# Eight heads per tile: sliding-window K and V loaded in 64 KB rows, each tile in two 64-partition transfers

## The chip, the cores and the metric

The kernel runs on one core of one Trainium2 chip; the chip's other cores are not used. The metric is the device time of the program in microseconds. The kernel is written in Bass with a recording layer of its own: every operation is recorded with what it reads and writes, semaphores are worked out from that, and then each engine's list is emitted in the recorded order. Five engines take part: TensorE (PE, with its weight loads as PEld), VectorE (DVE), ScalarE (ACT), GpSimd (POOL) and SyncE (SP). SP does nothing but issue the large loads, in program order, each behind its waits.

## The reference

Two independent attention layers, A and B, decode one token, and their outputs are concatenated. Both have 32 heads of width 128, a model width of 512, and caches of 16,384 positions in bfloat16. A attends to all positions, B only to the last 4,096.

```python
def _B_ref(x, k_cache, v_cache, wq, wo):           # A: the same with W = Sk
    W = min(4096, max(256, Sk // 4))
    q = (x @ wq) ... [heads, 1, 128]
    k, v = k_cache[:, :, Sk - W:, :], v_cache[:, :, Sk - W:, :]
    scores = einsum("bhqd,bhkd->bhqk", q, k) * (Dh ** -0.5)
    o = einsum("bhqk,bhkd->bhqd", softmax(scores), v)
    return o.reshape(B, Sq, Hq * Dh) @ wo

return concatenate([A(...), B(...)], axis=-1)
```

K and V are read once: A has 2 x 134.2 MB, B 2 x 33.6 MB in its window (67.1 MB in all), and the four weight matrices 4.2 MB each.

## The kernel before

**Units and tiles.** The work is cut into 20 units, each with a K tile and a V tile of 8 MB: 128 partitions, 256 positions (`2 * CH`) of 128 values per partition. A unit of A holds two heads: 64 partitions each, and a partition holds 256 consecutive positions of one head, a 64 KB row of the cache. A has 16 units. A unit of B holds eight heads as two parts of four: part `u` is positions `u * CH` to `(u + 1) * CH` of the tile's free dimension, and within it partition `4 * i + h` holds 128 positions of head `h`, a 32 KB row. B has 4 units. The order of units is B0, then A0 to A15, then B1 to B3.

**Buffers.** Two K buffers (`KS`) in turn, and one V buffer (`VS`). An 8 MB tile of A is one DMA transfer; a tile of B is two of 4 MB, one for each part (`b_window`, `load_k_half`, `load_k`, `load_v`). The first unit's two K parts are loaded around A's `wq`, the last unit's V parts go one into the free K buffer (`VL0`, behind A's `wo`) and one into `VS` (`VL1`), and B's `wo` follows in five pieces of 16, 8, 4, 3 and 1 rows (`wo_pieces`, line 765).

**What a unit does.** DVE multiplies K by the head's q in two products (`scores_prod`, line 437, one for each half of the free dimension), adds up along the 128 values in a tree of four additions (line 449) and a reduction (line 456), and takes the maximum per partition (line 465). PE turns the maxima into a row, DVE takes the maximum per head and spreads it (`max_all`, lines 488 and 489), PE turns it back. ACT makes the exponentials with their sums (line 516) and writes them into `pm` once for each head of the tile, masked so that a head keeps only its own partitions (`spread_p`, line 502). PE multiplies `pm` by V (`pv`, line 564), ACT scales and evicts (line 576), PE picks the heads' columns (`columns`, line 586), ACT stores them (line 595). The softmax and PV of a unit are recorded between the two products and the tree of the next unit.

**What a load waits for.** K of unit T + 1 waits until DVE has finished the tree of unit T - 1 (`free_k`, line 461). V of unit T - 1 is issued after the column store of unit T - 2 (line 595), so that VS is free. SP's order is V of T - 1, K of T + 1, V of T, and so on. In a unit of B, the first product waits for the first K transfer alone, the second product for the second; PV waits for both V transfers.

**The end.** The last unit's V is multiplied the other way round, into columns (`pv_columns`, line 604), part 0 from the K buffer into `oc_t`, part 1 from `VS` into `OC2`, each normalised by DVE (line 611). Then the heads' outputs are permuted (`permute_o`), multiplied by `wo` piece by piece (line 656), summed (line 665), turned (line 669) and stored.

Of the kernel before, what the change touches and what calls it, by code (L numbers as in the profile page):

```python
# [12 lines left out]
P = 128  # L13
# [18 lines left out]
class _Stream:  # L32
# [13 lines left out]
    def __init__(self, tc):  # L46
        self.tc, self.nc = tc, tc.nc
        nc = tc.nc
        self.eng = {"PE": nc.tensor, "DVE": nc.vector, "ACT": nc.scalar, "SP": nc.sync, "POOL": nc.gpsimd}
        self.ops = {e: [] for e in self.eng}  # L50
        self.known = {e: {} for e in self.eng}
        self.writer, self.readers = {}, {}
        self.sems, self.tokens, self.counts, self.taken = {}, {}, {}, set()
        self.loop = {}

    def sem(self, name):
# [16 lines left out]
    def op(self, eng, emit, r=(), w=(), dma=None, tok=None, takes=()):  # L73
        assert all(k in self.writer or "." in k for k in r), r
        known = self.known[eng]
# [152 lines left out]
def kernel(  # L228
# [21 lines left out]
    inv = 1.0 / math.sqrt(DH)  # L250
    assert SkA == P // 2 * 2 * CH and WB == P // 4 * CH

# [15 lines left out]
    ident = sb("ident", [P, P], BF16)  # L268
    one_f = sb("one_f", [1, 1], F32)
    one_b = sb("one_b", [1, 1], BF16)  # L270
    ones_col = sb("ones_col", [P, 1], F32)
    pick = sb("pick", [HQ, P + 4], BF16)
    sc = sb("sc", [P, 2 * CH], F32)
    m_t = sb("m", [P, 2], F32)
    M_t = sb("M", [1, 8], F32)
    Mr = sb("Mr", [1, 2 * P], F32)
    bias = sb("bias", [P, 2], F32)
    p_t = sb("p", [P, 2 * CH], BF16)
    cs = sb("cs", [P, 2], F32)
    csm = sb("csm", [P, 8], F32)  # L280
    pm_t = sb("pm", [P, 2 * CH * 4], BF16)
    r_t = sb("r", [P, 8], F32)
# [7 lines left out]
    A, B = _Side(), _Side()  # L290
    for s, n, x, wq, wo, nh in ((A, "A", A_x, A_wq, A_wo, 2), (B, "B", B_x, B_wq, B_wo, 4)):
        s.n, s.x, s.wq, s.wo, s.nh, s.parts = n, x, wq, wo, nh, nh // 2
        s.xT = sb(f"xT{n}", [P, KC], BF16)
        s.q = sb(f"q{n}", [P, HQ // nh, DH], BF16)
        s.O = sb(f"O{n}", [P, HQ], BF16)
        s.Op = sb(f"Op{n}", [P, HQ], BF16)
        s.mask = sb(f"mask{n}", [P, nh], F32)
        s.groups = 4 // s.parts
        s.rows = sb(f"rows{n}", [P, 8 * s.groups // nh, nh, 4], F32)
        s.sel = sb(f"sel{n}", [P, s.parts, nh * 4], F32)  # L300
        s.o = pst(f"o{n}")
# [6 lines left out]
    def by_head(s, ap):  # L308
        if s is A:
            return ap.rearrange("p (h i) -> p h i", h=s.nh)  # L310
        return ap.rearrange("p (i h) -> p h i", h=s.nh)

    def b_window(cache, g):
        return cache[0, 4 * g : 4 * g + 4, SkB - WB : SkB, :].rearrange("h (i l) d -> i h (l d)", l=CH)

# [18 lines left out]
    def load(dst, src, w, dma, tok=None):  # L334
        st.op("SP", lambda: L.dma_start(out=dst, in_=src), w=w, dma=dma, tok=tok)  # L335

    def load_k_half(un, u):
        load(flat(un.K[:, u * CH : (u + 1) * CH, :]), b_window(B_k_cache, 2 * un.g + u),
             [f"k{un.k}{u}"], f"K{un.k}{u}")

    def load_k(un):
        if un.s is A:
            load(flat(un.K[:, :, :]), a_pair(A_k_cache, un.g), [f"k{un.k}0", f"k{un.k}1"], f"K{un.k}0")
# [24 lines left out]
    def make_masks(s):  # L368
        n = s.n
        st.op("DVE", lambda: V.tensor_reduce(out=s.mask[:, :], in_=by_head(s, identf[:, :]), axis=AX.X, op=ALU.add),  # L370
              r=["identf"], w=["mask" + n])
# [11 lines left out]
    def spread_x(s, area, key):  # L383
# [16 lines left out]
        for j in range(s.nh):  # L400
            dst = s.xb[:, j, :, :]
            if s is A:
                dst = dst.rearrange("p c (h i) -> p c h i", h=s.nh)[:, :, j, :]
            else:
                dst = dst.rearrange("p c (i h) -> p c i h", h=s.nh)[:, :, :, j]
            st.op("DVE", lambda dst=dst: V.tensor_copy(dst, s.xT[:, :].unsqueeze(2).broadcast_to([P, KC, P // s.nh])),
                  r=["xT" + s.n, key], w=[f"{key}.{j}"])
# [20 lines left out]
    def scores_prod(un, u):  # L428
        s = un.s
        k = un.K[:, u * CH : (u + 1) * CH, :]  # L430
        j = un.g if s is A else 2 * un.g + u
# [44 lines left out]
    def max_all(un):  # L476
        s, n = un.s, un.s.parts
        w = n * s.nh
        if s is A:
            rows, wide = by_head(s, sm[0:1, 0:P]), by_head(s, Mr[:, 0:P])  # L480
            Mv = M_t[:, 0:w]
            spread = Mv.unsqueeze(2).broadcast_to([1, s.nh, P // s.nh])
        else:
            rows = sm[0:1, 0 : n * P].rearrange("p (v i h) -> p v h i", v=n, h=s.nh)
            wide = Mr[:, 0 : n * P].rearrange("p (v i h) -> p v h i", v=n, h=s.nh)
            Mv = M_t[:, 0:w].rearrange("p (v h) -> p v h", v=n)
            spread = Mv.unsqueeze(3).broadcast_to([1, n, s.nh, P // s.nh])
        st.op("DVE", lambda it=None: V.tensor_reduce(out=Mv, in_=rows, axis=AX.X, op=ALU.max), r=["sm_r"], w=["M"], takes=["smr"])  # L488
        st.op("DVE", lambda it=None: V.tensor_copy(wide, spread), r=["M"], w=["Mr"], tok="Mr")

        def turn():
            for v in range(n):
                i = T_.matmul(  # L493
                    sm[:, 256 + v : 257 + v], lhsT=Mr[:, v * P : (v + 1) * P], rhs=one_f[:, :],
                    start=True, stop=True,
                )
            return i

        st.op("PE", turn, r=["Mr", "one_f"], w=["sm_c"], takes=["Mr"], tok="smc")

# [55 lines left out]
    def pv(un):  # L556
# [14 lines left out]

        st.op("PE", mms, r=["v0", "v1"] + [f"pm0.{j}" for j in range(4)], w=["o" + s.n], takes=["V0"] if s is A else ["V0", "V1"], tok="pv")

# [24 lines left out]

    def pv_columns(un, v, V_t, vk, ps, pk, pmk, takes):
        s = un.s  # L600

        def mms():
            for l in range(un.n):
                x = T_.matmul(
                    ps[:, 0 : s.nh], lhsT=V_t[:, l, :], rhs=un.pm[:, (v * un.n + l) // 4, :, l % 4],
                    start=(l == 0), stop=(l == un.n - 1),
                )
            return x

        st.op("PE", mms, r=[vk] + [f"{pmk}.{j}" for j in range(4)], w=[pk], takes=takes)  # L610
        st.op("DVE", lambda: V.tensor_tensor(
            out=s.O[:, un.col(v) : un.col(v) + s.nh], in0=ps[:, 0 : s.nh],
            in1=r_t[:, v * s.nh : (v + 1) * s.nh], op=ALU.mult,
        ), r=[pk, "r"], w=[f"O{s.n}.{un.col(v)}"])

# [61 lines left out]

    x0 = 4 * KC * P
    x_pieces = ((0, D // 4), (D // 4, D // 2), (D // 2, D))
# [14 lines left out]
    ), r=["identf0"], w=["identf"])  # L694
    for t, key, val in ((one_f, "one_f", 1.0), (one_b, "one_b", 1.0), (ones_col, "ones_col", 1.0),
                        (A.o, "oA", 0.0), (B.o, "oB", 0.0)):
# [12 lines left out]
    st.op("SP", lambda: L.dma_start(out=flat(KS[1][:, :, :]), in_=a_pair(A_k_cache, 0)),  # L709
          w=["k10", "k11", *(f"x{n}.{a}" for n in "AB" for a, _ in x_pieces)] + [f"k10.{j}" for j in range(4)], dma="K10")  # L710

    parts = []
    for T, un in enumerate(units):
# [5 lines left out]
        if un.last:  # L719
# [55 lines left out]
    recip(un)  # L775
    pv_columns(un, 0, W[:, CH : 2 * CH, :], wk + "1", oc_t, "oc", "pm0", ["pm"])
# [38 lines left out]
```

## Time and profile before

The median of three runs is 824.38 us (824.25 to 824.51). The profiled execution took 824.25 us; its span, from the first to the last instruction, is 822.5 us.

| | |
|---|---|
| span of the profiled execution | 822.5 us |
| DVE busy | 750.4 us (91%) |
| PE busy | 197.9 us (24%), weight loads 99.0 us (12%) |
| ACT busy | 60.0 us (7%) |
| read from HBM | 352.32 MB |
| DVE products, lines 437 | 40 of 8.68 us |
| DVE trees, line 449 | 84 operations, 333.3 us |

How to read it: the page's second part cuts the span into 40 equal slices, and each digit is a busy share in tenths; its DMA row is the mean busy share of sixteen DMA engines, and the GB/s row what they moved. The list of DMA issues names tile and tensor, how many such transfers there were, their size, and the median time from issue to landing, which includes what stood ahead in the queue. In the chain that ended last, each step is followed back to what released it. The trace also keeps the packets of the DMA queues and the marks with which a transfer's sixteen shares report their completion. Timeline rows give start, duration, engine, line and operation.

### The profile page before, as it was taken

The numbers are of one execution on the slowest core, as the hardware profiler recorded it, in microseconds if no ns is written. First come the engines' busy times: TensorE is split into PE (matmuls) and PEld (weight loads), VectorE is DVE, ScalarE is ACT, GpSimd is POOL, SyncE is SP. The second block draws the span as 40 slices with busy tenths as digits, with TensorE's granted clock in tenths as the row PEclk, the third lists the DMA queues.
The fourth block names the chain that finished last, engine by engine and source line by source line (L and its number), as shares of the span: only waits on it lengthen the run. The fifth ranks groups of instructions, "written<-read, shape, count | busy, mean of one in ns | idle before, by whom it ended". The sixth has DMA issues, their size and how long they took to land. (4 is left out here: it accounts for less than half of the span.)

```text
span 822.5 us, 5105 instructions
## 1 busy us (share of the span) xinstructions
PE 197.9 (24%) x1985; PEld 99.0 (12%) x1985; DVE 750.4 (91%) x258; ACT 60.0 (7%) x168; POOL 0.7 (0%) x6
## 2 busy tenths in 40 slices
PE   3401212203030303030303212030303030303176
PEld 1100101101010101010101101010101010101035
DVE  2999899999999999999999999999999999999960
ACT  0101000001010100000000001010100000010111
POOL 0000000000000000000000000000000000000000
PEclk9765656565565655565655565555656555655575
DMA  9999999999999999999999999999999999999997
GB/s 383 433 433 433 457 412 450 418 447 421 444 424 441 427 437 430 437 430 437 430 437 430 437 430 437 430 437 430 437 430 437 430 422 445 422 433 431 432 432 298
DMA packets 8094, 352.44 MB, mean 429 GB/s; under 512 B 915, under 2 KB 1046, under 8 KB 1302
## 3 DMA queue, kind: packets, MB, share of 16 engines
q1 hardware_dynamic: 8072, 352.33, 99.2%
q8 instruction: 6, 0.10, 0.0%
q14 instruction: 2, 0.02, 0.0%
q10 hardware_dynamic: 14, 0.00, 0.0%
HBM read 352.32 MB, written 0.00 MB: 428 GB/s over the span
## 5 line engine op out<-in xcount | busy, mean ns | idle before, releaser
L449 DVE TENSOR_TENSOR k<-k 128x16384 bf16<-128x16384 bf16 (+3 forms) x84 | 333.3, 3968 | 2.2
L437 DVE TENSOR_TENSOR k<-k,qA 128x16384 bf16<-128x16384 bf16 x32 | 277.8, 8682 | 21.2 <-DVEq L122 21.1
L564 PE MATMUL oA<-v,pm 128*8 128x512 bf16 x1024 | 89.4, 525 | 111.0 <-PEq L122 111.0
L437 DVE TENSOR_TENSOR k<-k,qB 128x16384 bf16<-128x16384 bf16 x8 | 69.4, 8679 | 1.0 <-DVEq L122 1.0
L471 PE MATMUL sm<-identf,m 128*1 128x128 f32 x24 | 8.1, 369 | 207.8 <-PEq L122 207.8
L493 PE MATMUL sm<-one_f,Mr 1*128 1x1 f32 x48 | 12.4, 335 | 188.8 <-PEq L122 188.8
L564 PEld LDWEIGHTS oA<-v,pm 128*8 128x8 bf16 x1024 | 30.1, 110 | 163.7 <-issue 155.3
L456 DVE TENSOR_REDUCE sc<-k 128x256 f32<-128x2048 bf16 (+1 forms) x21 | 45.9, 2185 | 0.7
L493 PEld LDWEIGHTS sm<-one_f,Mr 1*128 1x128 f32 x48 | 11.2, 300 | 195.1 <-issue 195.1
L512 ACT ACTIVATE bias<-sm 128x1 f32<-128x1 f32 (+1 forms) x20 | 3.4, 171 | 412.0 <-ACTq L122 412.0
L471 PEld LDWEIGHTS sm<-identf,m 128*1 128x1 f32 x24 | 1.7, 80 | 209.7 <-issue 209.7
L576 ACT ACTIVATE osb<-oA,r 128x512 f32<-128x512 f32 x16 | 11.0, 687 | 214.1 <-ACTq L122 214.1
L564 PE MATMUL oB<-v,pm 128*16 128x512 bf16 x192 | 17.6, 546 | 23.1 <-PEq L122 23.1
L586 PE MATMUL oc<-selA,osb 128*128 128x2 f32 x128 | 16.4, 250 | 15.6 <-PEq L122 15.6
L586 PEld LDWEIGHTS oc<-selA,osb 128*128 128x128 f32 x128 | 15.5, 191 | 23.2 <-issue 23.2
L544 PE MATMUL sm<-cs,rowsA 128*128 128x1 f32 x32 | 8.9, 348 | 32.3 <-PEq L122 32.3
L502 ACT ACTIVATE pm<-p,maskA 128x256 bf16<-128x256 bf16 x32 | 14.5, 500 | 0.5
L544 PEld LDWEIGHTS sm<-cs,rowsA 128*128 128x128 f32 x32 | 8.0, 311 | 33.2 <-issue 33.2
L419 PE MATMUL tp<-v,osb 128*128 128x512 bf16 x32 | 9.1, 454 | 10.6 <-DMA v<-in_A_wq_dram 10.6
L516 ACT ACTIVATE p<-sc,bias 128x256 bf16<-128x256 f32 (+1 forms) x24 | 11.3, 470 | 0.6
L488 DVE TENSOR_REDUCE M<-sm 1x2 f32<-1x128 f32 (+1 forms) x20 | 6.0, 298 | 5.8 <-DVEq L122 5.8
L465 DVE TENSOR_REDUCE m<-sc 128x1 f32<-128x256 f32 (+1 forms) x20 | 8.4, 420 | 2.8
(73 smaller groups left out, 108.0 us busy)
## 6 DMA issues: line engine op xcount, KB each, us to landing
k<-in_B_k_cache_dram SPq DMA_DIRECT2D x8, 4096.0 KB, 35.9
v<-in_B_v_cache_dram SPq DMA_DIRECT2D x7, 4096.0 KB, 29.3
v<-in_B_wq_dram SPq DMA_DIRECT2D x1, 4096.0 KB, 12.2
v<-in_A_wq_dram SPq DMA_DIRECT2D x1, 4096.0 KB, 30.5
k<-in_A_wo_dram SPq DMA_DIRECT2D x1, 4096.0 KB, 33.5
k<-in_B_v_cache_dram SPq DMA_DIRECT2D x1, 4096.0 KB, 42.9
v<-in_B_wo_dram SPq DMA_DIRECT2D x1, 2048.0 KB, 25.1
v<-in_B_wo_dram SPq DMA_DIRECT2D x1, 1024.0 KB, 27.0
```

The costliest lines, as they stand in the source:

```text
L419: x = T_.matmul(out_ap, lhsT=s.xb[:, j, c, :], rhs=wq[:, c, j, g : g + 4, :], start=(k == 0), stop=(k == n - 1),)
L437: return V.tensor_tensor(out=k, in0=k, in1=s.q[:, bass.ds(i, 1), :].broadcast_to([P, CH, DH]), op=ALU.mult)
L449: st.op("DVE", lambda it=None, w=w: V.tensor_tensor(out=k[:, :, 0:w], in0=k[:, :, 0:w], in1=k[:, :, w : 2 * w], op=ALU.add), r=keys, w=keys)
L456: st.op("DVE", lambda it=None: V.tensor_reduce(out=sc[:, l0:l1], in_=un.K[:, l0:l1, 0:8], axis=AX.X, op=ALU.add), r=[f"k{un.k}{u}" for u i ...
L471: i = T_.transpose(sm[0:1, v * P : (v + 1) * P], m_t[:, v : v + 1], identf[:, :])
L493: i = T_.matmul(sm[:, 256 + v : 257 + v], lhsT=Mr[:, v * P : (v + 1) * P], rhs=one_f[:, :], start=True, stop=True,)
L502: return S.activation(out=out, in_=in_, func=ACT.Copy, scale=mask)
L516: st.op("ACT", lambda it=None, v=v: S.activation(out=p_t[:, v * n : (v + 1) * n], in_=sc[:, v * n : (v + 1) * n], func=ACT.Exp, scale=inv, ...
L544: i = T_.matmul(sm[v * w : (v + 1) * w, 264:265], lhsT=s.rows[:, :, :, :].rearrange("p r a b -> p (r a b)"), rhs=cs[:, v : v + 1], start=T ...
L564: x = T_.matmul(s.o[r0 : r0 + un.rows, :], lhsT=un.pm[:, l, :, :].rearrange("p a b -> p (a b)"), rhs=VS[:, 4 * l : 4 * l + 4, :], start=(i ...
L576: st.op("ACT", lambda it=None: S.activation(out=osb[:, :], in_=s.o[:, :], func=ACT.Copy, scale=r_t[:, 0:1]), r=["o" + s.n, "r"], w=["osb"] ...
L586: x = T_.matmul(oc_t[:, 0:w], lhsT=osb[:, j * P : (j + 1) * P], rhs=sel[:, j, :], start=(j == 0), stop=(j == 3),)
```

## The change

B's tile is laid out anew. It still holds eight heads, but each partition now holds 256 consecutive positions of one head, as in A: a 64 KB row of the cache. Partitions 0 to 63 hold heads 0 to 3 of the tile (partition `4 * i + h`), partitions 64 to 127 heads 4 to 7. One transfer fills one half of the partitions, over the whole free dimension (`load_b`, `b_window`); the key of each tile is split into `.a` and `.b` for the recording layer (`halves`). Where half a tile is loaded (the first unit's K, the last unit's V), it is half of the positions, in two transfers of 2 MB with 32 KB rows each. The first product of a B unit waits for both transfers of its tile. A unit of B has one part with eight heads (`nh` 8, `parts` 1): one q row set of four groups, one maximum and one exponential per partition, eight masked copies into `pm` (which doubles in size), 32 weight columns in `pv`, one accumulation over both V halves in `pv_columns` and one normalisation (`norm_columns`). The one-element tile `one_f` is dropped in favour of a slice of `ones_col`.

```diff
+        self.halves = {k: [k + ".a", k + ".b"] for k in ("k00", "k01", "k10", "k11", "v0", "v1")}
...
+        r, w = ([x for k in ks for x in self.halves.get(k, [k])] for ks in (r, w))
...
-    assert SkA == P // 2 * 2 * CH and WB == P // 4 * CH
+    assert SkA == P // 2 * 2 * CH and WB == P // 8 * 2 * CH
...
-    pm_t = sb("pm", [P, 2 * CH * 4], BF16)
+    pm_t = sb("pm", [P, 2 * CH * 8], BF16)
...
-    for s, n, x, wq, wo, nh in ((A, "A", A_x, A_wq, A_wo, 2), (B, "B", B_x, B_wq, B_wo, 4)):
-        s.n, s.x, s.wq, s.wo, s.nh, s.parts = n, x, wq, wo, nh, nh // 2
+    for s, n, x, wq, wo, nh in ((A, "A", A_x, A_wq, A_wo, 2), (B, "B", B_x, B_wq, B_wo, 8)):
+        s.n, s.x, s.wq, s.wo, s.nh, s.parts = n, x, wq, wo, nh, 1
...
-    def b_window(cache, g):
-        return cache[0, 4 * g : 4 * g + 4, SkB - WB : SkB, :].rearrange("h (i l) d -> i h (l d)", l=CH)
+    def b_window(cache, g, half, l0, l1):
+        h = 8 * g + 4 * half
+        rows = cache[0, h : h + 4, SkB - WB : SkB, :].rearrange("h (i l) d -> i h (l d)", l=2 * CH)
+        return rows[:, :, l0 * DH : l1 * DH]
...
+    def load_b(dst, cache, un, l0, l1, key, sems, toks=(None, None)):
+        for half, x in enumerate("ab"):
+            load(flat(dst[half * 64 : half * 64 + 64, :, :]), b_window(cache, un.g, half, l0, l1),
+                 [f"{k}.{x}" for k in key], sems[half], toks[half])
+
     def load_k_half(un, u):
-        load(flat(un.K[:, u * CH : (u + 1) * CH, :]), b_window(B_k_cache, 2 * un.g + u),
-             [f"k{un.k}{u}"], f"K{un.k}{u}")
+        l0, l1 = u * CH, (u + 1) * CH
+        load_b(un.K[:, l0:l1, :], B_k_cache, un, l0, l1, [f"k{un.k}{u}"], [f"KF{u}a", f"KF{u}b"])
...
-            for u in (0, 1):
-                load_k_half(un, u)
+            load_b(un.K, B_k_cache, un, 0, 2 * CH, keys, sems)
...
-            for u in (0, 1):
-                load(flat(VS[:, u * CH : (u + 1) * CH, :]), b_window(B_v_cache, 2 * un.g + u),
-                     [f"v{u}"], f"V{u}", f"V{u}")
+            load_b(VS, B_v_cache, un, 0, 2 * CH, ["v0", "v1"], ["V0", "V1"], ["V0", "V1"])
...
         st.op("DVE", mul, r=[kk, f"q{s.n}{j // 4}"], w=[kk],
-              takes=[f"K{un.k}{u}"] if s is B or u == 0 else [])
+              takes=[] if u or un is units[0] else [f"K{un.k}0"] if s is A else [f"K{un.k}0", f"K{un.k}1"])
...
-            load(flat(W[:, CH : 2 * CH, :]), b_window(B_v_cache, 2 * un.g), [wk + "1"], "VL0")
+            load_b(W[:, CH : 2 * CH, :], B_v_cache, un, 0, CH, [wk + "1"], ["VL0a", "VL0b"])
...
-    load(flat(VS[:, 0:CH, :]), b_window(B_v_cache, 2 * un.g + 1), ["v0"], "VL1")
+    load_b(VS[:, 0:CH, :], B_v_cache, un, CH, 2 * CH, ["v0"], ["VL1a", "VL1b"])
...
-    pv_columns(un, 1, VS[:, 0:CH, :], "v0", OC2, "oc2", "pm1", ["pm1"])
+    pv_columns(un, CH, VS[:, 0:CH, :], "v0", "pm1", ["pm1"])
     parts.append(st.ops["PE"][-1])
+    norm_columns(un)
```

More of the change, by code (lines that the diff above doesn't have):

```diff
@@ L73, in op @@
     def op(self, eng, emit, r=(), w=(), dma=None, tok=None, takes=()):
-        assert all(k in self.writer or "." in k for k in r), r
+        r, w = ([x for k in ks for x in self.halves.get(k, [k])] for ks in (r, w))
         known = self.known[eng]
@@ L268 @@
     ident = sb("ident", [P, P], BF16)
-    one_f = sb("one_f", [1, 1], F32)
     one_b = sb("one_b", [1, 1], BF16)
     ones_col = sb("ones_col", [P, 1], F32)
+    one_f = ones_col[0:1, :]
     pick = sb("pick", [HQ, P + 4], BF16)
     sc = sb("sc", [P, 2 * CH], F32)
-    m_t = sb("m", [P, 2], F32)
+    m_t = sb("m", [P, 1], F32)
     M_t = sb("M", [1, 8], F32)
-    Mr = sb("Mr", [1, 2 * P], F32)
-    bias = sb("bias", [P, 2], F32)
+    Mr = sb("Mr", [1, P], F32)
+    bias = sb("bias", [P, 1], F32)
     p_t = sb("p", [P, 2 * CH], BF16)
-    cs = sb("cs", [P, 2], F32)
+    cs = sb("cs", [P, 1], F32)
     csm = sb("csm", [P, 8], F32)
-    pm_t = sb("pm", [P, 2 * CH * 4], BF16)
+    pm_t = sb("pm", [P, 2 * CH * 8], BF16)
     r_t = sb("r", [P, 8], F32)
@@ L310, in by_head, with heads @@
             return ap.rearrange("p (h i) -> p h i", h=s.nh)
-        return ap.rearrange("p (i h) -> p h i", h=s.nh)
-    def b_window(cache, g):
-        return cache[0, 4 * g : 4 * g + 4, SkB - WB : SkB, :].rearrange("h (i l) d -> i h (l d)", l=CH)
+        return ap.rearrange("p (b i h) -> p b h i", b=2, h=s.nh // 2)
+    def heads(s, ap):
+        return ap if s is A else ap.rearrange("p (b h) -> p b h", b=2)
+    def b_window(cache, g, half, l0, l1):
+        h = 8 * g + 4 * half
+        rows = cache[0, h : h + 4, SkB - WB : SkB, :].rearrange("h (i l) d -> i h (l d)", l=2 * CH)
+        return rows[:, :, l0 * DH : l1 * DH]
     def a_pair(cache, g):
@@ L335, in load @@
         st.op("SP", lambda: L.dma_start(out=dst, in_=src), w=w, dma=dma, tok=tok)
+    def load_b(dst, cache, un, l0, l1, key, sems, toks=(None, None)):
+        for half, x in enumerate("ab"):
+            load(flat(dst[half * 64 : half * 64 + 64, :, :]), b_window(cache, un.g, half, l0, l1),
+                 [f"{k}.{x}" for k in key], sems[half], toks[half])
     def load_k_half(un, u):
-        load(flat(un.K[:, u * CH : (u + 1) * CH, :]), b_window(B_k_cache, 2 * un.g + u),
-             [f"k{un.k}{u}"], f"K{un.k}{u}")
+        l0, l1 = u * CH, (u + 1) * CH
+        load_b(un.K[:, l0:l1, :], B_k_cache, un, l0, l1, [f"k{un.k}{u}"], [f"KF{u}a", f"KF{u}b"])
     def load_k(un):
+        keys, sems = [f"k{un.k}0", f"k{un.k}1"], [f"K{un.k}0", f"K{un.k}1"]
         if un.s is A:
-            load(flat(un.K[:, :, :]), a_pair(A_k_cache, un.g), [f"k{un.k}0", f"k{un.k}1"], f"K{un.k}0")
+            load(flat(un.K[:, :, :]), a_pair(A_k_cache, un.g), keys, sems[0])
         else:
-            for u in (0, 1):
-                load_k_half(un, u)
+            load_b(un.K, B_k_cache, un, 0, 2 * CH, keys, sems)
     def load_v(un):
@@ L369, in make_masks @@
         n = s.n
-        st.op("DVE", lambda: V.tensor_reduce(out=s.mask[:, :], in_=by_head(s, identf[:, :]), axis=AX.X, op=ALU.add),
+        st.op("DVE", lambda: V.tensor_reduce(out=heads(s, s.mask[:, :]), in_=by_head(s, identf[:, :]), axis=AX.X, op=ALU.add),
               r=["identf"], w=["mask" + n])
@@ L404, in spread_x @@
             else:
-                dst = dst.rearrange("p c (i h) -> p c i h", h=s.nh)[:, :, :, j]
+                dst = dst.rearrange("p c (b i h) -> p c b i h", b=2, h=s.nh // 2)[:, :, j // 4, :, j % 4]
             st.op("DVE", lambda dst=dst: V.tensor_copy(dst, s.xT[:, :].unsqueeze(2).broadcast_to([P, KC, P // s.nh])),
@@ L430, in scores_prod @@
         k = un.K[:, u * CH : (u + 1) * CH, :]
-        j = un.g if s is A else 2 * un.g + u
+        j = un.g
         kk = f"k{un.k}{u}"
@@ L477, in max_all @@
         s, n = un.s, un.s.parts
[L478 to L487, printed above, removed]
+        rows, wide = by_head(s, sm[0:1, 0:P]), by_head(s, Mr[:, 0:P])
+        Mv = heads(s, M_t[:, 0 : s.nh])
+        spread = Mv.unsqueeze(len(wide.shape) - 1).broadcast_to([*wide.shape])
         st.op("DVE", lambda it=None: V.tensor_reduce(out=Mv, in_=rows, axis=AX.X, op=ALU.max), r=["sm_r"], w=["M"], takes=["smr"])
@@ L493, in turn @@
                 i = T_.matmul(
-                    sm[:, 256 + v : 257 + v], lhsT=Mr[:, v * P : (v + 1) * P], rhs=one_f[:, :],
+                    sm[:, 256 + v : 257 + v], lhsT=Mr[:, v * P : (v + 1) * P], rhs=one_f,
                     start=True, stop=True,
@@ L497, in turn @@
             return i
-        st.op("PE", turn, r=["Mr", "one_f"], w=["sm_c"], takes=["Mr"], tok="smc")
+        st.op("PE", turn, r=["Mr", "ones_col"], w=["sm_c"], takes=["Mr"], tok="smc")
     def on_scalar(out, in_, mask):
@@ L570, in mms @@
             return x
-        st.op("PE", mms, r=["v0", "v1"] + [f"pm0.{j}" for j in range(4)], w=["o" + s.n], takes=["V0"] if s is A else ["V0", "V1"], tok="pv")
+        st.op("PE", mms, r=["v0", "v1"] + [f"pm0.{j}" for j in range(s.nh)], w=["o" + s.n], takes=["V0"] if s is A else ["V0", "V1"], tok="pv")
     def evict(un):
@@ L597, in columns, with pv_columns, norm_columns @@
         st.op("ACT", keep, r=["oc", "v0", "v1"], w=[f"O{s.n}.{un.col(0)}"], takes=["oc"], tok="of")
-    def pv_columns(un, v, V_t, vk, ps, pk, pmk, takes):
+    def pv_columns(un, l0, V_t, vk, pmk, takes):
         s = un.s
         def mms():
-            for l in range(un.n):
+            for l in range(CH):
                 x = T_.matmul(
-                    ps[:, 0 : s.nh], lhsT=V_t[:, l, :], rhs=un.pm[:, (v * un.n + l) // 4, :, l % 4],
-                    start=(l == 0), stop=(l == un.n - 1),
-                )
-            return x
-        st.op("PE", mms, r=[vk] + [f"{pmk}.{j}" for j in range(4)], w=[pk], takes=takes)
+                    oc_t[:, 0 : s.nh], lhsT=V_t[:, l, :], rhs=un.pm[:, (l0 + l) // 4, :, l % 4],
+                    start=(l0 + l == 0), stop=(l0 + l == un.n - 1),
+                )
+            return x
+        st.op("PE", mms, r=[vk] + [f"{pmk}.{j}" for j in range(s.nh)], w=["oc"], takes=takes)
+    def norm_columns(un):
+        s = un.s
         st.op("DVE", lambda: V.tensor_tensor(
-            out=s.O[:, un.col(v) : un.col(v) + s.nh], in0=ps[:, 0 : s.nh],
-            in1=r_t[:, v * s.nh : (v + 1) * s.nh], op=ALU.mult,
-        ), r=[pk, "r"], w=[f"O{s.n}.{un.col(v)}"])
+            out=s.O[:, un.col() : un.col() + s.nh], in0=oc_t[:, 0 : s.nh], in1=r_t[:, 0 : s.nh], op=ALU.mult,
+        ), r=["oc", "r"], w=[f"O{s.n}.{un.col()}"])
     def permute_o(s):
@@ L676 @@
     wo_pieces = (16, 8, 4, 3, 1)
-    x0 = 4 * KC * P
+    x0 = B.nh * KC * P
     x_pieces = ((0, D // 4), (D // 4, D // 2), (D // 2, D))
@@ L694 @@
     ), r=["identf0"], w=["identf"])
-    for t, key, val in ((one_f, "one_f", 1.0), (one_b, "one_b", 1.0), (ones_col, "ones_col", 1.0),
+    for t, key, val in ((one_b, "one_b", 1.0), (ones_col, "ones_col", 1.0),
                         (A.o, "oA", 0.0), (B.o, "oB", 0.0)):
@@ L709 @@
     st.op("SP", lambda: L.dma_start(out=flat(KS[1][:, :, :]), in_=a_pair(A_k_cache, 0)),
-          w=["k10", "k11", *(f"x{n}.{a}" for n in "AB" for a, _ in x_pieces)] + [f"k10.{j}" for j in range(4)], dma="K10")
+          w=["k10", "k11", *(f"x{n}.{a}" for n in "AB" for a, _ in x_pieces)] + [f"k10.{j}" for j in range(B.nh)], dma="K10")
     parts = []
@@ L775 @@
     recip(un)
-    pv_columns(un, 0, W[:, CH : 2 * CH, :], wk + "1", oc_t, "oc", "pm0", ["pm"])
+    pv_columns(un, 0, W[:, CH : 2 * CH, :], wk + "1", "pm0", ["pm"])
     parts.append(st.ops["PE"][-1])
-    pv_columns(un, 1, VS[:, 0:CH, :], "v0", OC2, "oc2", "pm1", ["pm1"])
+    pv_columns(un, CH, VS[:, 0:CH, :], "v0", "pm1", ["pm1"])
     parts.append(st.ops["PE"][-1])
+    norm_columns(un)
     mark = permute_o(B)
```

## The prediction

> **What bounds the kernel now.** I read the page first: its time slices, its queue totals, its chain of waits; then the list of DMA issues, the waits of DVE, and the timeline of the last units. The time slices come first:
>
> ```profile
> DVE  2999899999999999999999999999999999999960
> ...
> DMA  9999999999999999999999999999999999999997
> GB/s 383 433 433 433 457 412 450 418 447 421 444 424 441 427 437 430 437 430 437 430 437 430 437 430 437 430 437 430 437 430 437 430 422 445 422 433 431 432 432 298
> ```
>
> Two rows are full, DVE's and the DMA's. The DMA row never falls below nine tenths before the last slice, and the GB/s row stays at some 432 throughout, over A's tiles (middle) and B's (both ends). The queue part says whose traffic that is:
>
> ```profile
> q1 hardware_dynamic: 8072, 352.33, 99.2%
> ...
> HBM read 352.32 MB, written 0.00 MB: 428 GB/s over the span
> ```
>
> One queue, SyncE's, carries all of it. The chain that ended last agrees: it ends in a load.
>
> ```profile
> DMA 3%; SPq 0%; PE 0%; DVE 0%; issue 0%; ACT 0%
> DMA v<-in_B_wo_dram 3%; SPq L765 0%; PE oc L656 0%; SPq L335 0%; PE tp L669 0%; DVE p L671 0%; DVE cols L665 0%; ACT OB L595 0%
> ```
>
> The chain is short because the last load was issued early and stood behind others in the queue. What set its landing (818.27 us by its completion mark) is the sum of all bytes ahead of it. The list of issues shows that backlog:
>
> ```profile
> k<-in_B_k_cache_dram SPq DMA_DIRECT2D x8, 4096.0 KB, 35.9
> v<-in_B_v_cache_dram SPq DMA_DIRECT2D x7, 4096.0 KB, 29.3
> ...
> k<-in_A_k_cache_dram SPq DMA_DIRECT2D x16, 40.3
> v<-in_A_v_cache_dram SPq DMA_DIRECT2D x16, 30.6
> ```
>
> The last column is issue to landing. By completion marks an 8 MB tile of A lands 19.35 us after what was ahead of it and a 4 MB transfer of B 9.715 us. So of A's 40.3 us for K some 21 us are queue, of V's 30.6 some 11 us; at B's V issue of 709.82 us the queue still holds work until 721.25. Nothing runs dry. DVE is nearly as full, but it idles 21.2 us before A's products waiting for K. So: the time is bytes over rate, and a change counts by what it does to the rate.
>
> How the rate comes about: the packets in the trace form sixteen chains without gaps. A 64 KB packet takes 2.42 us, a 32 KB one 1.218: 27.0 GB/s in each chain, whatever the tensor, row length or other engines' work. The wo pieces with rows of 16 KB down to 1 KB hold the same pace (2 MB lands 4.9 us behind the one before, 128 KB 0.32). Cost follows bytes: a path of fixed width, sixteen times. Every such transfer goes to all 128 partitions, so each sixteenth stands for eight destination partitions: 3.38 GB/s per partition is the most the trace ever shows.
>
> **The change, part by part.** B's 67.1 MB stay 67.1 MB. Before: 16 transfers of 4 MB, 128 partitions in 32 KB rows, 16 x 9.715 = 155.4 us of the stream. After: 20 transfers, each into 64 partitions. Six tiles (K of units 1 to 3 in B, V of units 0 to 2) come in 64 KB rows, two (first K, last V) in quarters of 2 MB with 32 KB rows.
>
> *Rows and packets.* A's 19.35 us against 2 x 9.715 = 19.43 prices 64 KB rows: 0.08 us x 6 tiles = 0.48 us less. Four more issues of some 0.54 us lie on SP's queue, 11 us or more ahead of need: nothing. 16 more 4-byte completion packets for each take 9 ns apiece: nothing.
>
> *Half the partitions.* This is the term that decides, and no row of the trace has it; the nearest are 128-partition transfers. Lower bound: the sixteen paths belong to the movers, each takes its sixteenth of a 64-partition transfer at 27.0 GB/s, cost 0 (less the 0.48). Upper bound: the paths belong to the destination, eight partitions each; then 64 partitions have eight paths, the transfer runs at 64 x 3.38 = 216 GB/s, and since the second half stands behind the first in the same queue, the other eight paths idle meanwhile. B's stream is then 2 x (155.4 - 0.48) = 309.8 us: +154.4. I take the upper one. Reason: time goes strictly with bytes, packets have no visible price of their own, and the chains, once 1 us out of step after a stall, stay so without catching up; that is what private, fixed paths at the end of the journey look like, and for the lower end a partition would have to take twice what any partition has taken in 352 MB. A queue served in order also gives the second half no way to use idle paths. This isn't proof; the other end keeps a chance.
>
> [...] No run here shows a 64-partition transfer.
>
> *Out of step.* Where two movers share a path and one is ahead by d, it has the path alone for d, and goes to the second half d earlier. That saves about d per half. Completion marks show the spread between the first and last sixteenth: 0.5 us until 100 us, 1.8 us after (single stalls of 1 us hit one chain each). For a pair taken at random I put a third of 0.5 (0.17) for the first 6 halves, and 0.67 for the other 14 (the chains stand in two clusters some 1.2 us apart, half of the pairs straddle them): 1 + 9.4 = 10 us less. Bounds: 0, and 3 + 25 = 28.
>
> *Waits on whole tiles.* K's two halves held different positions, and the first product of a B unit waited for its own alone. Now each half holds half of the partitions, so product 0 takes both. Timeline of before:
>
> ```profile
> 681.32 8.69 DVE L437 TENSOR_TENSOR k<-k,qB 128x16384 bf16<-128x16384 bf16 x1
> ...
> 718.62 8.68 DVE L437 TENSOR_TENSOR k<-k,qB 128x16384 bf16<-128x16384 bf16 x1
> ...
> 756.12 8.68 DVE L437 TENSOR_TENSOR k<-k,qB 128x16384 bf16<-128x16384 bf16 x1
> ```
>
> The second halves landed at 682.47, 721.25 and 760.10. At the old rate DVE would start 1.2, then 2.6, then 4.0 us late. Queued behind it are the trees, the release of K (SP's next K) and the maxima. The 21 us of queue ahead of a K cover that; the last unit's tree would end at 797 instead of 793.1, and its maximum waits anyway for PE, busy with A's output projection until 798.8. Cost nothing; without that cover 4 us. At the halved rate K arrives every 77 us or so against 37.5 us of DVE work: the wait is large, but it is the stream itself, already counted.
>
> *Engine work.* Per B unit ACT makes eight masked copies instead of four (0.43 us each: +1.7) and one exponential of 256 instead of two of 128 (-0.3); DVE's maxima shrink by some 0.4 us; PE does the same 64 matmuls with 32 weight columns instead of 16, and one transposition instead of two. PV comes 1.4 us later, so V's issue could; 11 us of queue cover it. Head: B's q is one group of 32 matmuls, its copy to SBUF ends at about 22.4 instead of 18.9, against the first K at 22.89: 0.5 us of cover. x is spread by a memset twice as long (+0.9) and eight copies: wq's landing at 13.18 covers it (DVE was done with x at 10.7). Tail: +1.3 us of masked copies on ACT, +0.75 on DVE, before V's last half lands (808.67), one normalisation instead of two. All covered by loads that land later; at the halved rate by more.
>
> *Sum.* Against the profiled execution's 824.25 us (span 822.5 and 1.8 around it; the runs' median of 824.38 is 0.1 above): 824.25 + 154.4 - 10 = 968.7, say **969 us**. The case's own range is 950 to 980. The 4 us after the last landing stay.
>
> **Rivals.**
> *No effect on the rate (the other side).* The movers are the limit. For it: the sixteen chains are what the trace shows, and it can't tell mover from destination. Against it: the doubled intake per partition. Time: 824.25 - 0.5 = 823.8, within 0.2% of before (1.65 us, about what a measurement of this kernel can tell). Faster by more than that would need 0.27 us per 64 KB-row tile instead of 0.08, in six places; slower by more, a cover above that fails (the 4 us of DVE).
> *Uneven sharing.* Two movers on a path don't share evenly, one runs a good part of a half ahead, and both sets of paths then work at once. The gain is the lead per half: with 3 to 5 us, 20 x 3 to 5 = 60 to 100 off, 878 to 918; all between 845 and 945 I count here. For it: chains keep a lead once they have it. Against it: no chain runs away from the rest over 800 us, but they don't share paths there.
> *The later product becomes the bound.* It would need the last tree to end after 798.8; at the old rate it lacks 1.7 us, at the new one it isn't near. No chance of its own.
>
> **Numbers.** Forecast 0.72, uneven sharing 0.08, no effect on the rate 0.20, split into 0.14 within 0.2%, 0.03 faster and 0.03 slower through a failed cover. Slower 0.72 + 0.08 + 0.03 = 0.83. The range takes in the forecast and the uneven sharing, 845 to 982; the no-effect case, 2 in 10, is left out.
>
> **What would show it.** Right: GB/s in the slices of B's loads falls to 215 to 235 while the DMA share stays at nine; A's slices stay at 432; DVE's share falls to about 77% with waits for K in B's products; a pair of B's transfers lands 37 to 39 us after what was ahead of it; the chain still ends in wo. Wrong: B's slices at 432 and a span of 822; or B's at 260 to 350, which is uneven sharing; or gaps in the DMA row, which would be a wait that I took for covered.

## The result, and the profile after

The changed kernel takes 995.6 us (median of six runs, 992.8 to 1001.1), against 824.3 us before: a ratio of 1.209, interval 1.207 to 1.211. The direction and the place were as forecast, the size was not: 969 us with a range up to 982. The profiled execution took 1001.05 us, the longest of the six, with a span of 999.0; a second profile of the same kernel (below) fell at 994.5 us. Ratios leave out slow runs, which are over 1.5% above a kernel's fastest: only two of the four of `lead` below, the profiled one among them, at the same granted clock as its other two (0.58).

The time slices of the changed kernel, to be held against those of before:

```profile
DVE  2659829999999999999999999999909449029200
...
DMA  9999999999999999999999999999999999999995
GB/s 294 293 337 252 247 423 439 436 428 436 434 431 430 439 430 433 436 428 433 441 425 430 446 422 433 446 422 433 239 247 336 210 210 210 210 210 198 274 210 181
```

The DMA row is as full as it was, so nothing ran dry: the DMA engines were busy all the time, and moved half as much while B's halves came in. The slices with nothing but B's halves in them read 210 GB/s, one of them 198; A's slices still read 433 on the mean; the slices between (337, 336, 274) are those where a transfer into all partitions stands among halves. DVE, full before, has its holes at both ends, where B's tiles are loaded. The queue part:

```profile
q1 hardware_dynamic: 7368, 352.33, 98.8%
...
HBM read 352.32 MB, written 0.00 MB: 353 GB/s over the span
```

The same bytes on the same queue, in 704 packets fewer. What waits has moved to DVE. Before, its list of waits began so (total, times, longest; `DVEq` is DVE's own sequencer, here at the semaphore of K's load):

```profile
DVE k L437 <- DVEq L122: 22.1, 17, 2.4
```

Now it begins so:

```profile
DVE k L446 <- DVEq L123: 136.7, 19, 42.7
DVE OB L616 <- PE oc L606: 28.1, 1, 28.1
DVE M L490 <- DVEq L123: 27.7, 1, 27.7
DVE k L446 <- DMA k<-in_B_k_cache_dram: 20.3, 2, 11.2
```

In the list of issues, A's tiles stand as long as they did, B's about twice as long, and A's `wo`, which comes behind B's, 84.7 us instead of 33.5:

```profile
k<-in_A_wo_dram SPq DMA_DIRECT2D x1, 4096.0 KB, 84.7
...
k<-in_A_k_cache_dram SPq DMA_DIRECT2D x16, 40.3
v<-in_A_v_cache_dram SPq DMA_DIRECT2D x16, 30.8
...
v<-in_B_v_cache_dram SPq DMA_DIRECT2D x6, 61.2
k<-in_B_k_cache_dram SPq DMA_DIRECT2D x6, 77.6
```

By completion marks, a 4 MB half lands 20.04 us after the one before it (872.20, 892.24, 912.28), where 4 MB took 9.715 before. A 64 KB packet takes 5.01 us on the mean in these halves (4.59 to 5.11 between 795 and 930 us) and 2.42 in A's tiles.

### The profile page after: what moved, and what is told of

It reads as the page before. It is cut to its first block, busy times and chain, and to the rows that moved or that the text cites. A ratio compares the mean times of both kernels' runs of the same rounds, so it can differ in the third digit from the quotient of the medians.

```text
span 999.0 us, 5086 instructions
## 1 busy us (share of the span) xinstructions
PE 199.7 (20%) x1967; PEld 99.8 (10%) x1967; DVE 751.3 (75%) x263; ACT 64.2 (6%) x174; POOL 0.7 (0%) x6
## 5 line engine op out<-in xcount | busy, mean ns | idle before, releaser
L566 PE MATMUL oA<-v,pm 128*8 128x512 bf16 x1024 | 93.1, 543 | 117.9 <-PEq L123 117.9
L495 PE MATMUL sm<-ones_col,Mr 1*128 1x1 f32 x40 | 10.8, 338 | 283.7 <-PEq L123 283.7
L495 PEld LDWEIGHTS sm<-ones_col,Mr 1*128 1x128 f32 x40 | 9.7, 300 | 289.2 <-issue 289.2
L514 ACT ACTIVATE bias<-sm 128x1 f32<-128x1 f32 x20 | 3.4, 172 | 485.3 <-ACTq L123 485.3
L566 PE MATMUL oB<-v,pm 128*32 128x512 bf16 x192 | 16.8, 525 | 75.4 <-PEq L123 75.4
L566 PEld LDWEIGHTS oB<-v,pm 128*32 128x32 bf16 x192 | 7.0, 126 | 83.9 <-issue 82.4
L504 ACT ACTIVATE pm<-p,maskB 128x256 bf16<-128x256 bf16 (+1 forms) x32 | 12.3, 470 | 0.1
## 6 DMA issues: line engine op xcount, KB each, us to landing
k<-in_A_wo_dram SPq DMA_DIRECT2D x1, 4096.0 KB, 84.7
```

What stands on the lines that cost most here:

```text
L495: i = T_.matmul(sm[:, 256 + v : 257 + v], lhsT=Mr[:, v * P : (v + 1) * P], rhs=one_f, start=True, stop=True,)
L504: return S.activation(out=out, in_=in_, func=ACT.Copy, scale=mask)
L566: x = T_.matmul(s.o[r0 : r0 + un.rows, :], lhsT=un.pm[:, l, :, :].rearrange("p a b -> p (a b)"), rhs=VS[:, 4 * l : 4 * l + 4, :], start=(i ...
```

## The experiments

All are edits of the changed kernel unless said otherwise. Times are medians, with the ratio to the kernel before on the same chip.

### Is it the loads, or the eight-head units?

`layout_only` keeps all of the changed computation and loads B's tiles as before:

```diff
     def load_b(dst, cache, un, l0, l1, key, sems, toks=(None, None)):
-        for half, x in enumerate("ab"):
-            load(flat(dst[half * 64 : half * 64 + 64, :, :]), b_window(cache, un.g, half, l0, l1),
-                 [f"{k}.{x}" for k in key], sems[half], toks[half])
+        if l1 - l0 == CH:
+            load(flat(dst[:, :, :]), b_window(cache, 2 * un.g + l0 // CH), key, sems[0])
+            return
+        for u in (0, 1):
+            load(flat(dst[:, u * CH : (u + 1) * CH, :]), b_window(cache, 2 * un.g + u), [key[u]], sems[u], toks[u])
```

Expected: 

> Changed kernel in all of its computation (eight heads per unit, first product behind both transfers), but B's tiles loaded as before: 4 MB transfers into 128 partitions in 32 KB rows, four heads each. The masks expect other heads on the partitions, so the outputs of B are not those of the reference. If the loads alone cost the time: 823.5 to 825.5 us, B at 432 GB/s. If the eight-head units or the wait for the whole tile cost something that the slow loads hide: 826 to 830 us.

Measured: 824.38 us, ratio 1.000 (0.999 to 1.001). Its row of GB/s is that of before, slice by slice:

```profile
GB/s 383 433 433 433 457 412 450 418 447 421 444 424 441 427 437 430 437 430 437 430 437 430 437 430 437 430 437 430 437 430 437 430 422 445 422 433 431 432 432 298
```

So at the old rate the eight masked copies, the later first product, the doubled memset and the longer tail cost nothing, as the prediction had them. All of the change's time is in the loads.

### Is it the halves, or the layout in HBM?

`split_before` is the kernel before, its four-head tiles and 32 KB rows kept, each 4 MB transfer cut into two of 64 partitions:

```diff
+        return rows[16 * half : 16 * half + 16]
+
+    def load_b(dst, cache, g, key, sem, tok=None):
+        for half, x in enumerate("ab"):
+            load(flat(dst[half * 64 : half * 64 + 64, :, :]), b_window(cache, g, half),
+                 [f"{key}.{x}"], sem + x, tok and tok + x)
...
-                load(flat(VS[:, u * CH : (u + 1) * CH, :]), b_window(B_v_cache, 2 * un.g + u),
-                     [f"v{u}"], f"V{u}", f"V{u}")
+                load_b(VS[:, u * CH : (u + 1) * CH, :], B_v_cache, 2 * un.g + u, f"v{u}", f"V{u}", f"V{u}")
```

Expected: 

> Kernel before, its layout of four heads and 32 KB rows kept, each 4 MB transfer of B cut into two of 2 MB into partitions 0 to 63 and 64 to 127. If the halves alone are the cause: B's 2 MB transfers land 9.9 to 10.1 us apart, 985 to 1005 us. If the layout is the cause: 824 to 830 us.

Measured: 989.3 us, ratio 1.200 (1.199 to 1.202); most of its 2 MB transfers land 9.7 to 9.9 us apart, where 4 MB took 9.715. Cutting the transfers is enough to lose the time, with nothing of the new layout.

`one_transfer` is the other way round: the new layout, eight heads and 64 KB rows, in one transfer into all 128 partitions.

```diff
-        h = 8 * g + 4 * half
-        rows = cache[0, h : h + 4, SkB - WB : SkB, :].rearrange("h (i l) d -> i h (l d)", l=2 * CH)
+        h = 8 * g
+        rows = cache[0, h : h + 8, SkB - WB : SkB, :].rearrange("h (i l) d -> i h (l d)", l=2 * CH)
...
+        load(flat(dst[:, :, :]), b_window(cache, un.g, l0, l1), key, sems[0], toks[0])
```

Expected: 

> Changed kernel with each B tile as one transfer into all 128 partitions (partition 8*i + h, 64 KB rows), everything else as changed. If the halves of the partitions are the cause (paths at the destination): B's tiles land 19.35 us apart, GB/s 432 throughout, 823 to 825 us. If the 64 KB rows of eight heads or the eight-head units are the cause: stays near 995 us.

Measured: 1000.2 us, ratio 1.212 (1.210 to 1.214). The simple theory, that 64 partitions are slow and 128 fast, failed: a transfer into all 128 partitions is as slow.

```profile
GB/s 288 291 307 288 210 446 428 427 444 430 428 441 427 433 440 425 435 440 425 435 443 422 435 443 422 435 443 422 249 246 338 210 228 210 215 218 202 262 207 157
```

V of B0 lands 40.4 us behind the transfer ahead of it (83.92, 124.30), where A's 8 MB take 19.35. The sharpest pair is the first K load: 4 MB in 32 KB rows into 128 partitions in both kernels, as 32 x 4 rows before (9.7 us) and as 16 x 8 rows here (19.9 us, 14.09 to 33.97). Size, row length and partitions are the same; what differs is the shape of the source and with it, presumably, which partitions belong to one sixteenth. The pitch of the rows in HBM differs too (64 KB instead of 32 KB), but it isn't the cause: `split_before` is slow at the old pitch (9.7 to 9.9 us for 2 MB), and the middle of `middle` below is nearly at full pace at the new one (10.9 us for 4 MB).

### How many partitions, or which?

`quarters` cuts each transfer into four of 32 partitions, `middle` into 32, 64 and 32:

```diff
-        for half, x in enumerate("ab"):
-            load(flat(dst[half * 64 : half * 64 + 64, :, :]), b_window(cache, un.g, half, l0, l1),
...
+    cuts = [(0, 32, 0, 2), (32, 64, 2, 4), (64, 96, 4, 6), (96, 128, 6, 8)]
...
+        for (p0, p1, h0, h1), x in zip(cuts, "abcd"):
+            load(flat(dst[p0:p1, :, :]), b_window(cache, un.g, h0, h1, l0, l1),
```

This is `quarters`. In `middle` the list of cuts (first and last partition, first and last head) is

```diff
+    cuts = [(0, 32, 0, 2), (32, 96, 2, 6), (96, 128, 6, 8)]
```

Expected of `quarters`: 

> Changed kernel with each B transfer cut further, into partitions 0 to 31, 32 to 63, 64 to 95 and 96 to 127, two heads each; which heads land on which partitions differs, so the outputs of B are not those of the reference. If a transfer's pace goes by the number of its partitions (3.38 GB/s each, as the prediction put its bound): B at 108 GB/s, some +470 us, near 1290 us. If it goes by eight shared paths which 32 partitions reach as well as 64: B at 210 GB/s, 990 to 1005 us.

Measured: 1000.0 us, ratio 1.213 (1.211 to 1.215). Its GB/s row, B's slices at both ends:

```profile
GB/s 290 291 335 260 210 455 423 425 449 425 428 444 425 434 441 425 436 441 422 438 438 425 438 438 422 441 436 425 252 218 352 205 207 210 210 210 210 260 211 206
```

The same 210 GB/s into 32 partitions as into 64, so a partition takes 6.6 GB/s here, twice what any had taken before. The pace doesn't go by the number of partitions.

Expected of `middle`: 

> Changed kernel with each B tile in three transfers: partitions 0 to 31, 32 to 95, 96 to 127 (two, four and two heads; which heads land on which partitions differs, so the outputs of B are not those of the reference). If half of the partitions at a time is slow whichever they are: 64 partitions at 210 GB/s here too, 990 to 1005 us. If it matters which partitions, and 32 to 63 with 64 to 95 reach all sixteen paths: the middle 64 land at 9.7 us for 4 MB, the outer quarters at 20 us for both, B's stream 155 + 80 us, 900 to 915 us.

Measured: 964.3 us, ratio 1.170 (1.168 to 1.172), between the two forecasts. The early tiles decide what it shows: V of B0 lands at 85.30 (partitions 0 to 31), 96.23 (32 to 95) and 105.77 us (96 to 127). The outer 2 MB took 10.1 and 9.5 us, half pace as in `quarters`; the 4 MB of the middle took 10.9, near the 9.7 of full pace. The stretch of that tile reads:

```profile
84.00:97.00 13.00, 1.11 (x4) 0.99 (x4) 12.97 (x6) 4.07 (x11) 0.00 (x0) 0.50 0.97 328
```

(the last column is GB/s: 328 over a stretch that is 11 us of the middle and the ends of two quarters). The middle has as many partitions as a half, and the same 16 x 4 shape and pitch at the source; only the place differs (and which four heads it holds). So it matters which partitions. The time is well above the sum of 900 to 915 because in the late tiles the sixteenths drifted up to 25 us apart and the middle lost its pace with it (11.7 us for 4 MB at 710.73, 20.9 at 845.24).

Side by side, 4 MB took 20.0 us into partitions 0 to 63 or 64 to 127, 2 MB some 10.0 into a quarter, and 4 MB 10.9 into partitions 32 to 95. Which partitions a sixteenth writes, in `one_transfer` or elsewhere, no run here shows.

### Would both halves at once help?

`two_queues` issues the second half of each tile from ScalarE's queue, from V of B1 on:

```diff
-                 [f"{k}.{x}" for k in key], sems[half], toks[half])
+                 [f"{k}.{x}" for k in key], sems[half], toks[half], "ACT" if half and both_queues[0] else "SP")
...
+        both_queues[0] = T >= NA + 2
```

Expected: 

> Changed kernel, only that from V of B1 on the second half of each tile (partitions 64 to 127) is issued from ScalarE's queue instead of SyncE's, so both halves can be under way at once. If the queue's order is what keeps half of the paths idle: those five tiles' loads run at up to 430 GB/s, 72 us less at best, 925 to 960 us. If the sixteen engines alternate between the queues in step, all on one half and then all on the other: the time stays at 990 to 1003 us.

Measured: 996.7 us, ratio 1.210 (1.208 to 1.212): no time gained.

```profile
GB/s 292 296 321 274 211 447 433 428 426 451 423 428 430 447 425 435 430 441 425 438 435 433 428 435 443 425 430 433 280 211 377 211 208 211 214 211 227 245 212 220
```

Different halves are under way at once now, if not of the same tile at first: from 834 to 858 us the first half of V of B1 (SyncE, landing at 867.17) beside the second of K of B3 (ScalarE, 864.12), from 892 to 916 us both halves of V of B2. In these two stretches a 64 KB packet takes 4.73 and 4.63 us on the mean instead of 5.01: 6 to 8% faster, and far from the 430 GB/s of the first forecast. By the last landing (989.42 us, against 988.41 in the second profile of the changed kernel) nothing is left of it. The packets also show the second of the two forecasts at work: all sixteen that are under way belong to SyncE's queue at 838 us, to ScalarE's at 843, to SyncE's at 847 and to ScalarE's at 852. The DMA engines go from queue to queue nearly together. So the order within one queue was not what held B's halves at half pace.

### What a lead is worth

The prediction's upper bound has sixteen engines on eight paths for a half; call two engines that would share a path a pair. No trace shows a path or who writes where, so what is said of pairs from here on is the author's reading of packets and landings. If the two of a pair are out of step by half a tile, one should write the first half of the partitions while the other writes the second. `lead` forces that once, in K of B2, by a transfer of 8 x 4 rows, which only eight engines share (its completion comes in eight shares, that of the other tiles in sixteen); the last number of a cut is the count of its rows `i`:

```diff
+    HALVES = [(0, 64, 0, 4, 16, "ab"), (64, 128, 4, 8, 16, "c")]
+    LEAD = [(0, 32, 0, 4, 8, "a"), (32, 64, 2, 4, 16, "b"), (64, 128, 4, 8, 16, "c")]
...
+            load_b(un.K, B_k_cache, un, 0, 2 * CH, keys, f"KB{un.k}", cuts=LEAD if un.g == 2 else HALVES)
```

Expected: 

> Changed kernel with K of B2 in three transfers: partitions 0 to 31 as 8 x 4 rows, which only eight of the sixteen engines can share (4 packets of 64 KB each), then partitions 32 to 63 as 16 x 2 rows and 64 to 127 as before (which rows of K lie on partitions 32 to 63 differs, so the outputs of B2's heads are not those of the reference). Eight engines thus fall 4 packets, one half of a tile, behind the other eight. If two engines that share a path keep a lead, from then on one writes the first half of the partitions while the other writes the second, and the three tiles V of B1, K of B3 and V of B2 take 9.7 to 10 us per half instead of 20: 55 to 60 us less, 930 to 945 us. If a lead is evened out when they meet, packets go back to 5.05 us within a tile: 985 to 1003 us.

Measured: 950 to 972 us in four runs, median 961.9, all shorter than any run of the changed kernel; ratio 1.158 (1.151 to 1.164). V of B1 and the first half of K of B3 land 12.0 us apart instead of 20 (810.25, 822.28, 834.35, 846.24), and the slices after the forced lead rise:

```profile
GB/s 283 305 316 272 218 431 428 423 425 430 436 436 436 436 433 430 427 436 436 436 433 436 436 436 436 436 430 433 425 256 218 368 223 348 332 343 210 267 262 43
```

```profile
810.00:846.00 36.00, 7.29 (x76) 4.22 (x76) 35.44 (x10) 4.92 (x13) 0.00 (x0) 0.59 0.98 346
```

346 GB/s with the very transfers that run at 210 in the changed kernel. By an estimate from the 2.42 us of a 64 KB packet in A's tiles, with four packets per half and a lead of L packets only 4 - L of them meet, so a half should take 2.42 x (8 - L) us. 12.05 is L = 3: by this estimate one packet of the forced four was lost. The gain doesn't last: the next half takes 13.7 us, and V of B2 18.8 and 20.0 (878.77, 898.72), while the first engine's marks stay 12 to 15 us apart, which speaks for some pairs having lost their lead. The chains end 19 us apart, and the forecast of 930 to 945 us was missed. `lead2` and `lead1` force two packets and one, by cutting that transfer to half and a quarter of the positions (`SPLIT` is 128 in `lead2`, 64 in `lead1`):

```diff
+    LEAD = [(0, 32, 0, 4, 8, "a"), (0, 32, 0, 2, 16, "d"), (32, 64, 2, 4, 16, "b"), (64, 128, 4, 8, 16, "c")]
+    SPLIT = 128
+            a, b = (l0, SPLIT) if xs == "a" else (SPLIT, l1) if xs == "d" else (l0, l1)
```

Expected of `lead2`: 

> As the kernel with the lead, but the transfer that only eight engines share holds half of the positions (2 packets' worth of 64 KB for each of the eight); the rest of those partitions follows as 16 x 2 rows (which rows of K lie on partitions 0 to 63 differs for B2). With 4 packets per half and a lead of L packets kept, a half takes 2.42 x (8 - L) us: 14.5 for L = 2, 17 if one of them is lost as in the first kernel (which showed 12.05, so L = 3). If leads are kept at any size: halves 14.5 to 17 us apart, 968 to 985 us. If only a large lead survives and a smaller one is evened out: 20.0 us, 985 to 1003 us.

Expected of `lead1`: 

> The same with a quarter of the positions, 1 packet's worth for each of the eight engines. If leads are kept at any size: halves 16.9 to 19.4 us apart, 978 to 993 us. If a lead of a packet or less is evened out, as the changed kernel's 20.04 us at a spread of 3 to 8 us suggests: 20.0 us, 988 to 1003 us.

Measured by the first engine's landing, the halves come 16.9 us apart in `lead2` (805.81, 822.69, 839.54, 856.49), which is L = 1 (16.9), and 19.2 in `lead1` (804.99, 824.26, 843.49, 862.73), L = 0 by the formula (19.4), though still 0.8 under the 20.0 of the changed kernel. By this estimate the lead left over each time was about a packet less than was forced. The last engines land 17 to 20 us apart in `lead2`, which speaks for some pairs not having it. In time nothing is left of it: 1000.5 us, ratio 1.212 (1.208 to 1.217), and 1003.3 us, ratio 1.215 (1.208 to 1.222). Both missed the times forecast for a lead that is kept. In `lead2` the chains end 17.5 us apart; `lead1` was profiled in the shortest of its four runs (994.2 us), so where the others lose time isn't shown.

### What being out of step costs

Completion marks of the changed kernel show three places where a transfer into all partitions took too long: V of A14, beside K of B1 (22.66 us for 8 MB instead of 19.35), V of A15 between two tiles of halves (23.44) and A's `wo` (15.28 for 4 MB instead of 9.72). `drain` lets the queue run empty once, ahead of B's late stage:

```diff
-            load_b(un.K, B_k_cache, un, 0, 2 * CH, keys, sems)
+            load_b(un.K, B_k_cache, un, 0, 2 * CH, keys, sems, r=["OA.28"] if un.g == 1 else ())
...
+            if un.s is B and un.g == 1:
+                load_k(un)
             load_v(prev)
-            if T + 1 < NT:
+            if T + 1 < NT and T != NA:
```

Expected: 

> Changed kernel, only that K of B1 (the first of B's late loads) waits until A14's columns are stored, so the queue runs empty for some 10 us and all sixteen chains of packets start B's stage together. If engines out of step lose time where halves meet transfers into all partitions (in the changed kernel V of A14 landed 3.3 us late, V of A15 4.1, A's wo 5.6, with 3 to 12 us between first and last sixteenth): the spread stays under 2 us, those losses fall to under 1 us each, and the time is 988 to 998 us in spite of the gap. If each such border costs by itself: losses of 3 to 5 us remain, 1003 to 1012 us. If a lead paid, as the prediction took it to: halves land later than 20.0 us apart without it, 1010 us or more.

Measured: 1003.9 us, ratio 1.218 (1.216 to 1.221). The gap shows in one slice:

```profile
DMA  9999999999999999999999999999599999999997
GB/s 291 295 337 252 244 426 423 443 428 430 439 428 435 436 427 435 435 430 435 435 430 435 435 430 435 433 433 435 134 210 378 236 210 212 215 212 205 275 214 230
```

V of A14 took 19.34, V of A15 19.42, A's `wo` 10.3 us: the losses are gone, 12.4 us of them, and the first and last sixteenth stay 0.9 to 1.7 us apart from K of B1 to V of B2. The gap cost 11.4 us (K of B1 lands 31.47 us behind the transfer ahead instead of 20.06). The forecast of 988 to 998 held for the mechanism and missed the time: the gap took back nearly all of the gain. The time falls in the range of the second case, but the losses, by which the cases differ, are those of the first. The halves stay at 20.0 us in step as out of step (19.9 to 20.2).

`after_again`, the changed kernel once more:

Expected: 

> Changed kernel as it is, once more. If its runs differ by how far the engines are out of step where halves meet transfers into all partitions, a profile near 995 us shows less than the 13 us that the one of 1001 us lost at V of A14, V of A15 and A's wo, and the same 20.0 us per half; if the pace of the halves differs from run to run, the 20.0 moves instead.

Measured: 994.5 us, ratio 1.206 (1.204 to 1.209). Its three places lose 1.9, 1.8 and 1.7 us, 5.4 in all against 13.0 in the profile of 1001.05 us: 7.6 us less, in a run that is 6.6 us shorter. Its halves come 20.07 us apart. These two runs differ by the borders, not by the pace. The loss is larger in the one where the sixteenths are further apart: at V of A14 3.3 us at a spread of 3.3 against 1.9 at 2.0, at A's `wo` 5.6 at 7.8 against 1.7 at 3.5.

## Why the prediction was wrong, step by step

Of its two bounds the prediction took the right one: the halves came at about half pace, 210 GB/s where A's tiles have 433, and one after the other, 20.04 us apart. That half of the partitions has half of the paths fits this, but no trace shows the paths. Three terms of the sum failed: the pace of a half, put at no loss beyond the factor of two; the lead, put at 10 us less; and the borders with transfers into all partitions, not in the sum at all.

**What bounds the kernel** was right: the bytes of one queue over its rate. `layout_only` shows that the costs put at nothing at the old rate were nothing.

**Half the partitions**: the right end was taken, but it was mis-sized, and in part taken for a false reason. The term was 2 x (155.4 - 0.48) = 309.8 us for B's stream; added up from completion marks it is 318.0 us in the first profile and 319.6 in the second, 8 to 10 more. The step that failed is that two engines on one path would share its 27.0 GB/s without loss: a packet of a half takes 5.01 us on the mean instead of 2 x 2.42 = 4.84, a half 20.04 instead of 19.4, which would be some 26.2 GB/s for a pair (an estimate, two packets of 64 KB in 5.01 us). The reason that "a partition would have to take twice what any partition has taken" fell with `quarters`, where partitions do just that (6.6 GB/s against 3.38). So the single partition wasn't the limit; that a group of partitions is fits `quarters` (210 GB/s into 32 as into 64) and `middle` (10.9 us for 4 MB into 32 to 95), but isn't shown. `one_transfer` shows that a transfer into all 128 can run at half pace as well (19.9 us for 4 MB).

**Out of step**: 10 us were taken off for leads, and none came. That a lead pays isn't what failed: forced in `lead`, by the estimate three packets of it left, it took 8 us off a half (12.0 instead of 20.0) for three halves. What failed is the estimate of the lead inside a pair from the spread over all sixteen. A half takes 20.04 to 20.07 us in the changed kernel, whatever the spread of 4 to 8.5 us, and 19.9 to 20.2 in `drain` at 0.9 to 1.7 us. No 64 KB packet between 795 and 930 us takes less than 4.59 us, where those of A's tiles take 2.42: read by pairs, the two engines of one are in step to within some tenths of a us, and the spread is between pairs (an estimate from these packets). By the formula the three lead runs each lost about a packet of lead, 2.4 us, which would swallow any lead that single stalls of 1 us make. Why it is lost isn't shown.

**The missing term**: nothing in the sum stood for the border between halves and transfers into all partitions. It would cost time if engines that are already in the next transfer write to paths that others still need; the losses that grow with the spread, and vanish in `drain`, fit that, but no trace shows who writes where. The borders cost 13.0 us at the three late borders in the first profile, 5.4 in the second, nothing at the first two of them and 0.6 at the third in `drain`, plus 0.7 at the early ones in the first.

The sum mended: 968.7 + 8.2 (pace) + 10 (no lead) + 13.7 (borders) = 1000.6 against 1001.05 us; for the second profile 968.7 + 9.8 + 10 + 5.4 = 993.9 against 994.5. The profile before has no row for either added cost, so the range had to leave room for them. It ended 3 us above the case of no lead (978.7), which left none for a half that takes more than twice the time or for a border.

**The rivals**: no effect on the rate is excluded. Uneven sharing doesn't happen by itself: the slices that it was to raise to 260 to 350 stay at 210. A lead that is forced does raise them, for a while (332 to 348 in three slices of `lead`). The later product never became a bound.

**What would show it**: A's slices at 433, a full DMA row and DVE's 75% (77 named) came as written; B's slices (210, where 215 to 235 were named) and a pair of halves (40.1 us instead of 37 to 39) missed by the slower packets (5.01 us against 4.84). The chain was to end in B's `wo`. In the second profile it does:

```profile
DMA v<-in_B_wo_dram 5%; SPq L769 0%; SPq L341 0%; PE oc L660 0%; PE tp L673 0%; DVE p L675 0%; DVE cols L669 0%; ACT OB L597 0%
```

In the first it reads

```profile
DMA v<-in_B_v_cache_dram 4%; PE oc L660 0%; PE oc L606 0%; SPq L341 0%; PE tp L673 0%; PE tp L624 0%; PE tp L629 0%; DVE p L675 0%; ACT p L625 0%; ACT OpB L636 0%; DVE cols L669 0%; DVE OB L616 0%; ACT OB L597 0%; DVEq L125 0%
```

because the last half of V lands at 985.25 us, 10.9 us behind its own first sixteenth, and the work on it ends at 990.42, just after the first 2 MB of `wo` land (990.12).

## What to carry to other kernels

Before a saturated load stream is cut or reshaped, time one transfer of the new shape, and don't go by its bytes, rows and partitions alone: 4 MB in 32 KB rows into all 128 partitions took 9.7 us here as 32 x 4 rows and 19.9 as 16 x 8. Price the bad case above the plain factor of two: packets of the halves lost another 3.5% here (5.01 us for 4.84), and a border with full transfers cost up to 5.6 us (A's `wo`, at a spread of 7.8 us between sixteenths; 1.7 us at 3.5). A saving that rests on engines being out of step should be counted only where a run has shown it: the 10 us taken off here didn't come.

## What was not expected of the hardware

A transfer of 16 x 8 rows into all 128 partitions ran at half pace (19.9 us for 4 MB), one of 32 x 4 rows into the same partitions at full pace (9.7 us). 64 partitions from 32 to 95 took 10.9 us for 4 MB, 64 from 0 or from 64 took 20.0. Two queues at once gained no time (996.7 us), while a forced lead brought the same transfers to 346 GB/s for three halves, before the next took 13.7 us and V of B2 18.8 and 20.0.
